# RWKV-5 attention followed by mixture of depths: weight loads re-cut and begun later, u and the gate vector as columns, state products on quarters, one PSUM buffer for the ranking's small results

## The chip, the cores and the metric

The kernel runs on one core of one Trainium2 chip. The metric is the device time in microseconds (us) of one execution; several executions give a median. A profile of one execution shows each instruction with its start, length and what it waited for.

## The reference

```python
batch, n_heads, seq, head_dim = (4, 8, 768, 48)
for t in range(S):
    kt, vt, rt = (k[:, :, t], v[:, :, t], r[:, :, t])
    cur = np.einsum('bhd,bhe->bhde', u[None] * kt, vt)
    y[:, :, t] = np.einsum('bhd,bhde->bhe', rt, state + cur)
    state = w[None, :, :, None] * state + np.einsum('bhd,bhe->bhde', kt, vt)
...
x = np.ascontiguousarray(attn_out.transpose(0, 2, 1, 3)).reshape(B, S, H * D)
scores = np.einsum('bsd,d->bs', x, w_gate)
out = x.copy()
for b in range(B):
    top_idx = np.argpartition(-scores[b], capacity)[:capacity]
    xe = x[b, top_idx]
    ye = np.maximum(xe @ w1, 0.0) @ w2
    g = 1.0 / (1.0 + np.exp(-scores[b, top_idx]))
    out[b, top_idx] = x[b, top_idx] + g[:, None] * ye
```

A linear recurrence per head, then, for the 128 (capacity) best tokens of each batch, an expert with 1024 hidden values (w1 is 384 x 1024, w2 is 1024 x 384). All data are float32.

## The kernel before

Time is cut into 24 units of 128 tokens, six per batch (NU = 24, NC = 6), each with all 8 heads in 4 pairs. The main loop (L571) handles unit n as follows; each engine runs its instructions in program order.

- PE: `states(n - 1)` (L312, what the state adds to y), `products(n)` (L277, key times value: what each half of the unit adds to the state), `scores(n)` (L286, key times query inside the unit), `values(n - 1)` (L331, scores times values), `turn(n + 1)` (L254, transposes of key and query), then ranking and expert work that the plan has put there.
- DVE: `added(n, 0)` (L299), `masked(n)` (L295), `added(n, 1)`, `turned(n + 1)`, `bonus_sum(n + 1)`, `score(n - 1)` (L366, the gate score), then comparisons for the ranking.
- POOL: `scaled(n + 2)` (L233, kw), `diagonal(n + 1)` (L251, at), `bonus(n + 2)` (L237 rk, L243 rku). About four instructions of 1.0 us or more in each unit.
- ACT: copies out of PSUM, the decay of the state (L310), the copy of y into x (L353 to L357).
- SP: issues nearly all DMAs, in order. `load(n + 4, part)` is held behind an instruction of unit n (the first `added`, `masked`, `turned`, `bonus_sum`), the weights behind `masked` and `score`, and the store of a unit's x behind ACT's copies. r, k and v come in rows of 192 bytes.

The products of a pair of heads (L282) use all 128 tokens as the contraction at once. The value tile `vpad` has 2 x 48 columns per head: the first half of the tokens has its values in the left 48 and zeros in the right, the second half the other way round, so that one product gives the sums of both halves side by side. The sums lie in the last 192 columns of the two PSUM banks of `rp`, the scores in the first 256.

[...] `rp` takes two, `y0` and `y1` two, and four go round under the name "m": transposed keys (pk) and queries (pr) in each unit, the transposed score row (`scores_along`, L375), the rank sums (`rank`, L396), the picked token numbers (`pick`, L434), the hidden layer (PH) and the expert's sum (PE, held over three units).

`plan(b)` (L528) puts the expert part of batch b on the units after it, with n = 6(b + 1): the score rows up to unit n + 1, the rank sums (`rank`) and the one-hot rows (`match`) in unit n + 2 ("turn"), `pick` and `fetch` (an indirect DMA on POOL's queue) in unit n + 3 ("bonus"), `chosen` in unit n + 5, then 8 hidden and 8 expert parts by MOVE: hidden 0 to 3 in unit n + 5, 4 and 5 in n + 6, 6 and 7 in n + 7, expert 0 to 2 in n + 8, 3 to 5 in n + 9, the last two in n + 10. Within a unit, "bonus" comes before "turn" and "turn" before "end". For the last batch all this is written out at the kernel's end.

`weights(j, behind)` (L166) loads piece j: pieces 0 to 7 are 128 hidden columns of w1 (all three row blocks, rows of 512 bytes), pieces 8 to 15 are 128 rows of w2 (1536 bytes each). Unit n issues pieces 2(n - 6) and 2(n - 6) + 1, that is in units 6 to 13. u and w_gate come as one row that is sent to all 128 partitions (L129, L557).

Before the loop, ACT clears the unused halves of `vpad` 2 to 5 (L153), PE runs 14 warm-up matmuls around `turn(0)`, and DVE makes the tables of powers of w.

Of the kernel before, what the change touches and what calls it, by code (L numbers as in the profile page):

```python
# [7 lines left out]
F32 = mybir.dt.float32  # L8
# [9 lines left out]
def kernel(  # L18
# [55 lines left out]
    for i, q in enumerate((nc.sync, nc.scalar)):  # L74
        q.dma_start(
            out=wp[i * PAD : i * PAD + D, 0, :],
            in_=bass.AP(tensor=w.tensor, offset=w.offset + i * D, ap=[[1, D], [2 * D, NP]]),
        )
    nc.scalar.activation(mark, mark, AF.Sigmoid)
    busy = const.tile([128, 512], BF16)  # L80
    nc.vector.memset(busy, 0.0)
# [34 lines left out]
    def held(dma, behind):  # L116
        if behind is not None:
            tc.add_manual_dep(dma.ins, behind.ins.name, wait_for, reason="loads come one by one")
# [7 lines left out]
            nc.gpsimd.memset(x[h * C : (h + 1) * C, :, (1 - h) * D : (2 - h) * D], 0.0)  # L126
    load(0, 0)
    load(0, 1)
    nc.sync.dma_start(out=ub, in_=bass.AP(tensor=u.tensor, offset=u.offset, ap=[[0, 128], [D, H], [1, D]]))  # L129
    load(0, 2)  # L130
    load(0, 3)
    load(1)
# [1 line left out]
    def warm(k):  # L134

        p = psum.tile([128, 512], F32, name="m", bufs=4)
        for _ in range(k):
            nc.tensor.matmul(out=p, lhsT=busy[:, :128], rhs=busy, start=True, stop=True)

    w1 = const.tile([128, KD, F], F32)  # L140
    w2 = const.tile([128, FB, Dm], F32)
# [6 lines left out]
    for x in rpads[2:]:  # L148
# [1 line left out]
    rp = psum.tile([128, 2, 512], F32, name="rp")  # L150
    nc.scalar.copy(rp[:, :, NP * C : NP * (C + D)].rearrange("t a (p d) -> t a p d", p=NP),
                   zt[:, None, :, :].to_broadcast([128, 2, NP, D]))
    for x in vpads[2:]:  # L153
        for h in range(2):
            rows = slice(h * C, (h + 1) * C)
            nc.scalar.copy(x[rows, :, (1 - h) * D : (2 - h) * D].rearrange("t (a p) d -> t a p d", a=2),  # L156
                           zt[rows, None, :, :].to_broadcast([C, 2, NP, D]))
    mask = const.tile([128, C], F32)
    dia = const.tile([128, C], F32)
    for c in range(2):  # L160
# [3 lines left out]
    causal = mask.bitcast(U32)[:, None, None, :].to_broadcast([128, 2, NP, C])  # L164

    def weights(j, behind):  # L166
        if 0 <= j < FB:
            f = slice(j * 128, (j + 1) * 128)
            held(nc.sync.dma_start(out=w1[:, :, f], in_=moe_w1.rearrange("(kd p) f -> p kd f", p=128)[:, :, f]), behind)
        elif FB <= j < 2 * FB:  # L170
            f = slice((j - FB) * 128, (j - FB + 1) * 128)
            held(nc.sync.dma_start(out=w2[:, j - FB, :], in_=moe_w2[f, :]), behind)


    tables = const.tile([128, 2, NP, T], F32)
# [98 lines left out]
    def turned(n, pr):  # L274
        return nc.vector.tensor_mul(RH[n][:CH], pr[:CH], tr[:CH])  # L275

    def products(n):  # L277

        for hp in range(NP):
            for i in range(2):  # L280
                at = NP * C + hp % 2 * 2 * D
                nc.tensor.matmul(out=rp[i * PAD : i * PAD + D, hp // 2, at : at + 2 * D],  # L282
                                 lhsT=kws[n % 3][:, 2 * hp + i, :D], rhs=VIN[n][:, 2 * hp + i, :],
                                 start=True, stop=True)

    def scores(n):  # L286
        for hp in range(NP):
# [11 lines left out]
    def added(n, c):  # L299
        z = ZA[n] if c == 0 else ZB[n]  # L300
        g = work.tile([128, NP, D], F32, name=f"g{c}", bufs=3)
        sums = rp[:, :, NP * C : NP * (C + D)].rearrange("d b (p e) -> d b p e", p=2)
        op = nc.vector.tensor_add(g.rearrange("d (b p) e -> d b p e", p=2), sums[:, :, :, c * D : (c + 1) * D],  # L303
                                  z.rearrange("d (b p) e -> d b p e", p=2))
        if c == 0:
            ZB[n] = g
            return op
        ZA[n + 1] = work.tile([128, NP, D], F32, name="z", bufs=3)
        for hp in range(NP):
            nc.scalar.activation(ZA[n + 1][:, hp, :], g[:, hp, :], AF.Copy, scale=wc[:, hp : hp + 1])  # L310
# [54 lines left out]
    def score(n):  # L365
        b, c = divmod(n, NC)  # L366
        return nc.vector.scalar_tensor_tensor(scr, xa[b][:, c, :], 1.0, wg, op0=OP.mult, op1=OP.mult,  # L367
                                              accum_out=sc[b][:, c : c + 1])
# [3 lines left out]
    spacer = const.tile([1, 1], F32)  # L372
    out_rows = out.rearrange("b s d -> (b s) d")

    def scores_along(b, j):  # L375
        p = psum.tile([128, 512], F32, name="m", bufs=4)
        nc.tensor.transpose(p[:, :128], sc[b][:, j : j + 1].to_broadcast([128, 128]), ident)
        SR[b, j] = p[:, :128]
        nc.scalar.copy(along[b % 2][:, j * 128 : (j + 1) * 128], SR[b, j])
# [16 lines left out]
    def rank(b):  # L396


        p = psum.tile([128, 512], F32, name="m", bufs=4)
        nc.tensor.matmul(out=p[:, NC - 1 : NC], lhsT=GT[b][:, 0, :128], rhs=ones[:, 1:2], start=True, stop=True)  # L400
        for c in range(NC - 1):
            for j in range(c + 1, NC):
                nc.tensor.matmul(out=p[:, c : c + 1], lhsT=GT[b][:, j, c * 128 : (c + 1) * 128], rhs=ones[:, 0:1],
                                 start=(j == c + 1), stop=(j == NC - 1))
        q = work.tile([128, NC], F32, name="qq")
        nc.vector.tensor_sub(q, QQ[b], p[:, :NC])
        QQ[b] = q
# [24 lines left out]
                nc.vector.tensor_scalar(oh[:, c, :], slots, q[:, c : c + 1], None, op0=OP.is_equal)  # L432

    def pick(b, z):  # L434
        p = psum.tile([128, 512], F32, name="m", bufs=4)
        for c in range(NC):
            nc.tensor.matmul(out=p[:, :5], lhsT=OH[b, z][:, c, :], rhs=tok[:, b * NC + c, :],
                             start=(c == 0), stop=(c == NC - 1))
        IDX[b, z] = work.tile([128, 1], I32, name="idx", bufs=NST + 1)
        with nc.allow_low_precision(reason="whole numbers below 2^24"):  # L440
            nc.vector.tensor_reduce(IDX[b, z], p[:, :2], axis=AX.X, op=OP.add)
        GA[b, z] = work.tile([128, 1], F32, name="gate", bufs=NST + 1)
        picked = work.tile([128, 1], F32, name="picked")
        nc.vector.tensor_reduce(picked, p[:, 2:5], axis=AX.X, op=OP.add)
        nc.scalar.activation(GA[b, z], picked, AF.Sigmoid)
# [71 lines left out]
    def step(n, where, f, *a):  # L517
        fill.setdefault((n, where), []).append((f, a))
# [9 lines left out]
    def plan(b):  # L528
        n = (b + 1) * NC
        for j in range(NC):  # L530
            step(n - NC + j + 2, "turn", scores_along, b, j)
            step(n - NC + j + 2, "turn", compare, b, j)
        step(n + 1, "turn", count, b)
        step(n + 1, "turn", parts_of_scores, b)
        step(n + 2, "turn", rank, b)
        for z in range(NST):
            step(n + 2, "turn", match, b, z)
            step(n + 3, "bonus", pick, b, z)
            step(n + 3, "bonus", fetch, b, z)
            step(n + 5, "scores", chosen, b, z)  # L540
        parts = [p for z in range(NST) for p in mlp(b, z)]
        for i, (f, a) in enumerate(parts):
            step(n + 5 + MOVE[i * 16 // len(parts)], "end", f, *a)
# [6 lines left out]
            f(*a)  # L550

    bonus(0)
    warm(10)
    pr = turn(0, k0, key_table)
    warm(4)
    load(2)
    nc.sync.dma_start(out=wg, in_=bass.AP(tensor=moe_w_gate.tensor, offset=moe_w_gate.offset, ap=[[0, 128], [1, Dm]]))  # L557
    load(3)
    turned(0, pr)
    bonus_scaled(0, nc.vector)  # L560
# [8 lines left out]
    scaled(1)  # L569
    bonus(1)  # L570
    for n in range(NU):  # L571
        if n == 2:
            late_tables()
        b, c = divmod(n, NC)
        if c == 0:
            ZA[n] = zt
        if n:
            behind = states(n - 1)
        products(n)
        scores(n)  # L580
        work_at(n, "scores")
        load(n + 4, 0, added(n, 0))
        op = masked(n)
        load(n + 4, 2, op)
        weights(2 * (n - NC), op)
        if n:
            values(n - 1, behind)
            finish(n - 1)
        if n + 1 < NU:
            pr = turn(n + 1)  # L590
        if c < NC - 1:
            added(n, 1)
        if n + 1 < NU:
            load(n + 4, 1, turned(n + 1, pr))
            load(n + 4, 3, bonus_sum(n + 1))
        if n + 2 < NU:
            scaled(n + 2)
        if n + 1 < NU:
            diagonal(n + 1)
        work_at(n, "bonus")  # L600
        if n + 2 < NU:
            bonus(n + 2)
        if n:
            weights(2 * (n - NC) + 1, score(n - 1))
        work_at(n, "turn")
        if n + 1 < NU:
            work_at(n, "end")
# [13 lines left out]

    some(2 * NST)
    behind = states(NU - 1)
    scores_along(last, NC - 2)
    compare(last, NC - 2)
    values(NU - 1, behind)
    finish(NU - 1)
    score(NU - 1)
    some(3 * NST)
    scores_along(last, NC - 1)  # L630
    compare(last, NC - 1)
    count(last)
    parts_of_scores(last)
    some(3 * NST)
    rank(last)
    for z in range(NST):
        match(last, z)
    some(2 * NST)
    for z in range(NST):
        pick(last, z)  # L640
        fetch(last, z)
    some(len(before) - NST)
# [38 lines left out]
```

## Time and profile before

| | |
|---|---|
| median of 3 runs | 164.13 us (163.67 to 168.28) |
| the profiled execution | 165.25 us, span 163.5 us |
| PE busy | 146.2 us (89%) |
| POOL busy | 117.7 us (72%) |
| DVE busy | 111.9 us (68%) |
| ACT busy | 76.5 us (47%) |
| DMA packets | 84323, of which 76480 under 512 B; 24.50 MB |
| SP's own queue of loads and stores | 62.8% of 16 engines' span |
| mean granted TensorE clock | 0.996 |

The span runs from the program's first instruction to its last. A busy share is a mean over stages with different limits. A row of a group tells the line, the engine, what is written from what, the shapes and the count, then busy us, mean ns of one, and the idle time just before. In a timeline, the first number is the start in us from the span's start, the second the length, and brackets at the end tell the idle time before an instruction and what ended it. In the chain of waits, each line is a start, a length and the engine and line that held up the end.

### The profile page before, as it was taken

To read this page: it belongs to the slowest core of one execution; us is meant where nothing else is said; L and a number is where in the kernel's file an instruction comes from. 1 tells how busy PE (TensorE), PEld (TensorE's weight loads), DVE (VectorE), ACT (ScalarE), POOL (GpSimd) and SP (SyncE) were. 2 spreads that over 40 slices of the span, in tenths; PEclk is the share of its full clock that TensorE was granted. 3 is DMA by queue.
4 is the path that set the end of the run, shared out by engine and by line. 5 is a ranking of instruction groups with operands and counts; after the bars stand their busy time and mean duration, and the time that the engine had idled before them with its cause. 6 is when DMAs were issued, how large, how long until landed. Compare 5 with 4: busy or idle time off the path is not lost.

```text
span 163.5 us, 7873 instructions
## 1 busy us (share of the span) xinstructions
PE 146.2 (89%) x3278; PEld 119.2 (73%) x3278; DVE 111.9 (68%) x352; ACT 76.5 (47%) x251; POOL 117.7 (72%) x156
## 2 busy tenths in 40 slices
PE   6969979997998866999998999999989999999970
PEld 2558868885787756999875779999676788858830
DVE  7856768889999956797898387488984857701010
ACT  6816666545664645167516344546643645102100
POOL 8499999999999996878799979688978431122002
PEclk9999999999999999999999999999999999999998
DMA  4998788888989989998999999988502212011001
GB/s 76 193 193 162 134 185 155 183 178 181 202 193 190 210 212 222 217 214 220 227 226 232 232 184 219 211 170 195 122 4 62 88 52 100 0 48 52 0 0 48
DMA packets 84323, 24.50 MB, mean 150 GB/s; under 512 B 76480, under 2 KB 83904, under 8 KB 84288
## 3 DMA queue, kind: packets, MB, share of 16 engines
q1 hardware_dynamic: 83568, 22.42, 62.8%
q0 software_dynamic: 512, 1.57, 2.9%
q8 instruction: 26, 0.43, 1.1%
q14 instruction: 9, 0.07, 0.1%
q10 hardware_dynamic: 208, 0.00, 0.1%
HBM read 18.48 MB, written 5.51 MB: 147 GB/s over the span
## 4 chain that ended last, share of the span: by engine, by line
PE 49%; POOL 20%; issue 13%; ACT 7%; DMA 6%; DVE 2%; POOLq 1%; SPq 0%; ACTq 0%; DVEq 0%
PE m L480 10%; PE m L489 7%; PE rp L282 7%; PE y L322 5%; PE rp L292 5%; POOL at L251 5%; PE m L260 4%; PE y L338 4%; POOL kw L233 4%; POOL rk L237 4%; POOL rku L243 4%; PE m L265 4%; DMA kin<-in_k_dram 3%; DMA rpad<-in_r_dram 3%; ACT vpad L156 2%
## 5 line engine op out<-in xcount | busy, mean ns | idle before, releaser
L251 POOL TENSOR_TENSOR at<-dia,du 128x512 f32<-128x512 f32 x24 | 30.0, 1249 | 7.4 <-DVE du L247 3.6
L237 POOL TENSOR_TENSOR rk<-rpad,kin 128x384 f32<-128x384 f32 x23 | 23.1, 1005 | 3.0 <-DMA rpad<-in_r_dram 2.9
L233 POOL TENSOR_TENSOR kw<-kin,wk 128x384 f32<-128x384 f32 x23 | 23.8, 1035 | 1.8 <-DMA kin<-in_k_dram 1.7
L243 POOL TENSOR_TENSOR rku<-rk,ub 128x384 f32<-128x384 f32 x23 | 23.1, 1004 | 1.8
L282 PE MATMUL rp<-vpad,kw 128*48 128x96 f32 x384 | 21.6, 251 | 2.9 <-POOL kw L233 1.2
L480 PE MATMUL m<-xt,w 128*128 128x128 f32 x192 | 23.2, 276 | 0.0
L489 PE MATMUL m<-w,ht 128*128 128x384 f32 x64 | 22.7, 492 | 0.1
L480 PEld LDWEIGHTS m<-xt,w 128*128 128x128 f32 x192 | 22.3, 192 | 0.6 <-ACT xt L471 0.5
L310 ACT ACTIVATE z<-g,wp 128x48 f32<-128x48 f32 x80 | 20.2, 325 | 4.8 <-DVE g L303 4.8
L355 ACT COPY x<-y 128x192 f32<-128x192 f32 x24 | 7.7, 320 | 27.4 <-PE y L338 26.6
L282 PEld LDWEIGHTS rp<-vpad,kw 128*48 128x48 f32 x384 | 16.3, 122 | 5.0 <-POOL kw L233 1.7
L275 DVE TENSOR_TENSOR rh<-m,tables 112x512 f32<-112x512 f32 x24 | 16.5, 686 | 4.5 <-PE m L265 4.5
L367 DVE SCALAR_TENSOR_TENSOR scr<-x,wg 128x384 f32<-128x384 f32 x24 | 17.9, 747 | 1.8 <-ACT x L357 1.8
L297 DVE COPY_PREDICATED at<-mask,rp 128x512 f32<-128x512 uint32 x24 | 17.6, 735 | 1.6 <-POOL at L251 1.6
L322 PE MATMUL y<-g,rh 48*64 48x48 f32 x384 | 16.7, 222 | 2.1 <-issue 1.2
L247 DVE TENSOR_REDUCE du<-rku 128x8 f32<-128x384 f32 x24 | 13.2, 549 | 6.5 <-POOL rku L243 6.3
L322 PEld LDWEIGHTS y<-z,rh 48*64 48x64 f32 x320 | 12.4, 134 | 6.8 <-issue 5.2
L292 PE MATMUL rp<-rh,kh 48*64 48x64 f32 x768 | 16.7, 224 | 0.0
L260 PE MATMUL m<-ident,kw 128*112 128x128 f32 x92 | 14.9, 285 | 1.8 <-POOL kw L233 1.8
L322 PE MATMUL y<-z,rh 48*64 48x48 f32 x320 | 15.7, 223 | 0.9 <-issue 0.9
L389 DVE TENSOR_SCALAR_CACHE_REDUCE gt<-along,sc 128x128 bf16<-128x128 f32 (+5 forms) x24 | 16.2, 676 | 0.2 <-issue 0.2
L292 PEld LDWEIGHTS rp<-rh,kh 48*64 48x64 f32 x768 | 13.4, 134 | 3.7 <-issue 0.7
(95 smaller groups left out, 250.7 us busy)
## 6 DMA issues: line engine op xcount, KB each, us to landing
rpad<-in_r_dram SPq DMA_DIRECT2D x24, 192.0 KB, 3.4
vpad<-in_v_dram SPq DMA_DIRECT2D x48, 96.0 KB, 4.4
out_dram<-x SPq DMA_DIRECT2D x24, 192.0 KB, 3.7
kin<-in_k_dram SPq DMA_DIRECT2D x23, 192.0 KB, 3.8
w<-in_moe_w_dram SPq DMA_DIRECT2D x16, 192.0 KB, 4.3
k<-in_k_dram SPq DMA_DIRECT2D x1, 192.0 KB
ub<-in_u_dram SPq DMA_DIRECT2D x1, 192.0 KB, 4.4
wg<-in_moe_w_gate_dram SPq DMA_DIRECT2D x1, 192.0 KB
```

What stands on the lines that cost most here:

```text
L233: nc.gpsimd.tensor_mul(kws[n % 3][:, :, :D], KIN[n], wk)
L237: nc.gpsimd.tensor_mul(rk, rpads[n % NIN][:, :, :D], KIN[n])
L243: engine.tensor_mul(RKU[n], RK[n], ub)
L251: nc.gpsimd.tensor_mul(AT[n], dia[:, None, :].to_broadcast([128, H, C]), DU[n].rearrange("t i p -> t (i p)")[:, :, None].to_broadcast([128 ...
L260: nc.tensor.transpose(pk[:CH, hp, :], two_heads(kws[n % 3] if keys is None else keys, hp), ident)
L282: nc.tensor.matmul(out=rp[i * PAD : i * PAD + D, hp // 2, at : at + 2 * D], lhsT=kws[n % 3][:, 2 * hp + i, :D], rhs=VIN[n][:, 2 * hp + i, ...
L292: nc.tensor.matmul(out=rp[ts, i, hp * C : (hp + 1) * C], lhsT=KH[n][rows, hp, ts], rhs=RH[n][rows, hp, ts], start=True, stop=True)
L310: nc.scalar.activation(ZA[n + 1][:, hp, :], g[:, hp, :], AF.Copy, scale=wc[:, hp : hp + 1])
L322: mm = nc.tensor.matmul(out=YP[n][i][j * C : (j + 1) * C, hp * D : (hp + 1) * D], lhsT=RH[n][rows, hp, c * C : (c + 1) * C], rhs=z[rows, h ...
L367: return nc.vector.scalar_tensor_tensor(scr, xa[b][:, c, :], 1.0, wg, op0=OP.mult, op1=OP.mult, accum_out=sc[b][:, c : c + 1])
L480: nc.tensor.matmul(out=ph[:, f % 4, :], lhsT=w1[:, d, f * 128 : (f + 1) * 128], rhs=XT[b, z][:, d, :], start=(d == 0), stop=(d == KD - 1))
L489: nc.tensor.matmul(out=pe[:, :Dm], lhsT=HT[b, z][:, f, :], rhs=w2[:, f, :], start=(f == 0), stop=(f == FB - 1))
```

## The change

The pieces of w1 are re-cut: six of 128 rows x 512 columns (2 KB per row, 256 KB each), one for each row block and half of the hidden columns. w2 stays in eight. The 14 pieces go out in units 8 to 15 by a table: one in unit 8, two in 9, one in 10 and two in each of 11 to 15; the first of a unit behind `masked`, the second behind `score`. The hidden parts 0 to 3 use the first three pieces, 4 to 7 the next three.

u and w_gate come as 128 x 3 columns, u over ACT's queue and w_gate over POOL's; PE's transposes spread a column over all partitions (`to_all`), and DVE (u) or ACT (w_gate) copies the result out of PSUM. The clearing of `vpad` 4 and 5 moves behind that copy, and the warm-up matmuls become 6 + 3 + 3.

In the last batch (units 18 to 23) `products` runs one product for each half of the tokens, with a contraction of 64 and 48 columns; each half of the tokens writes into its own bank. `added` reads accordingly.

`side()` gives one "m" buffer per loop iteration, shared by score row (columns 0 to 127), ranks (128 on) and picked (192 on). `rank` and `match` move from "turn" to "end" of their unit, behind expert parts of an earlier batch.

```diff
+    columns = const.tile([128, 2, KD], F32)
+    for i, (x, q) in enumerate(((u, nc.scalar), (moe_w_gate, nc.gpsimd))):
+        q.dma_start(out=columns[:, i, :], in_=bass.AP(tensor=x.tensor, offset=x.offset, ap=[[1, 128], [128, KD]]))
...
-    nc.sync.dma_start(out=ub, in_=bass.AP(tensor=u.tensor, offset=u.offset, ap=[[0, 128], [D, H], [1, D]]))
...
+    def to_all(i):
+
+        p = psum.tile([128, 512], F32, name="m", bufs=4)
+        for d in range(KD):
+            nc.tensor.transpose(p[:, d * 128 : (d + 1) * 128], columns[:, i, d : d + 1].to_broadcast([128, 128]), ident)
+        return p[:, :Dm]
...
+        if j < F // 512 * KD:
+            f, d = slice(j // KD * 512, (j // KD + 1) * 512), j % KD
+            held(nc.sync.dma_start(out=w1[:, d, f], in_=moe_w1[d * 128 : (d + 1) * 128, f]), behind)
+        else:
+            f = j - F // 512 * KD
+            held(nc.sync.dma_start(out=w2[:, f, :], in_=moe_w2[f * 128 : (f + 1) * 128, :]), behind)
+
+    NWP = F // 512 * KD + FB
+    DUE = {}
+    for j in range(NWP):
+        DUE.setdefault(2 * NC - 4 + (0, 1, 1, 2, 3, 3, 4, 4, 5, 5, 6, 6, 7, 7)[j * 14 // NWP], []).append(j)
...
+                if quarters(n):
+                    for c in range(2):
+                        ts, at = slice(c * C, (c + 1) * C), NP * C + hp * D
+                        nc.tensor.matmul(out=rp[to, c, at : at + D], lhsT=kws[n % 3][ts, h, :D],
+                                         rhs=VIN[n][ts, h, c * D : (c + 1) * D], start=True, stop=True)
...
+        if quarters(n):
+            op = nc.vector.tensor_add(g, sums[:, c].rearrange("d (p e) -> d p e", p=NP), z)
...
+    def side():
+
+        if 0 not in SIDE:
+            SIDE[0] = psum.tile([128, 512], F32, name="m", bufs=4)
+        return SIDE[0]
+
     def scores_along(b, j):
-        p = psum.tile([128, 512], F32, name="m", bufs=4)
+        p = side()
...
-        p = psum.tile([128, 512], F32, name="m", bufs=4)
+        p = side()[:, 128 : 128 + NC]
...
-        p = psum.tile([128, 512], F32, name="m", bufs=4)
+        p = side()[:, 192 : 192 + 5]
...
-        step(n + 2, "turn", rank, b)
+        step(n + 2, "end", rank, b)
         for z in range(NST):
-            step(n + 2, "turn", match, b, z)
+            step(n + 2, "end", match, b, z)
...
-    warm(10)
+    warm(6)
+    nc.vector.tensor_copy(ub, to_all(0).rearrange("t (h d) -> t h d", h=H))
+    warm(3)
     pr = turn(0, k0, key_table)
-    warm(4)
+    nc.scalar.copy(wg, to_all(1))
+    for x in vpads[4:]:
+        cleared(x)
+    warm(3)
...
     for n in range(NU):
+        SIDE.clear()
...
-        weights(2 * (n - NC), op)
+        weights_due(n, True, op)
...
-            weights(2 * (n - NC) + 1, score(n - 1))
+            weights_due(n, False, score(n - 1))
```

At the kernel's end `SIDE.clear()` stands ahead of each of the last batch's steps, so that there every step has a buffer of its own, as before.

More of the change, by code (lines that the diff above doesn't have):

```diff
@@ L152, with cleared @@
                    zt[:, None, :, :].to_broadcast([128, 2, NP, D]))
-    for x in vpads[2:]:
+    def cleared(x):
         for h in range(2):
@@ L157 @@
                            zt[rows, None, :, :].to_broadcast([C, 2, NP, D]))
+    for x in vpads[2:4]:
+        cleared(x)
     mask = const.tile([128, C], F32)
@@ L166, in weights, with weights_due @@
     def weights(j, behind):
[L167 to L172, printed above, removed]
+        if j < F // 512 * KD:
[8 more added lines that the diff above has]
+        DUE.setdefault(2 * NC - 4 + (0, 1, 1, 2, 3, 3, 4, 4, 5, 5, 6, 6, 7, 7)[j * 14 // NWP], []).append(j)
+    def weights_due(n, first, behind):
+        for j in DUE.get(n, [])[:1] if first else DUE.get(n, [])[1:]:
+            weights(j, behind)
     tables = const.tile([128, 2, NP, T], F32)
@@ L275, in turned, with quarters @@
         return nc.vector.tensor_mul(RH[n][:CH], pr[:CH], tr[:CH])
+    def quarters(n):
+        return n >= NU - NC
     def products(n):
@@ L280, in products @@
             for i in range(2):
[L281 to L284, printed above, removed]
+                h, to = 2 * hp + i, slice(i * PAD, i * PAD + D)
+                if quarters(n):
[3 more added lines that the diff above has]
+                                         rhs=VIN[n][ts, h, c * D : (c + 1) * D], start=True, stop=True)
+                else:
+                    at = NP * C + hp % 2 * 2 * D
+                    nc.tensor.matmul(out=rp[to, hp // 2, at : at + 2 * D], lhsT=kws[n % 3][:, h, :D],
+                                     rhs=VIN[n][:, h, :], start=True, stop=True)
     def scores(n):
@@ L301, in added @@
         g = work.tile([128, NP, D], F32, name=f"g{c}", bufs=3)
-        sums = rp[:, :, NP * C : NP * (C + D)].rearrange("d b (p e) -> d b p e", p=2)
-        op = nc.vector.tensor_add(g.rearrange("d (b p) e -> d b p e", p=2), sums[:, :, :, c * D : (c + 1) * D],
-                                  z.rearrange("d (b p) e -> d b p e", p=2))
+        sums = rp[:, :, NP * C : NP * (C + D)]
+        if quarters(n):
+            op = nc.vector.tensor_add(g, sums[:, c].rearrange("d (p e) -> d p e", p=NP), z)
+        else:
+            sums = sums.rearrange("d b (p e) -> d b p e", p=2)[:, :, :, c * D : (c + 1) * D]
+            op = nc.vector.tensor_add(g.rearrange("d (b p) e -> d b p e", p=2), sums,
+                                      z.rearrange("d (b p) e -> d b p e", p=2))
         if c == 0:
@@ L373 @@
     out_rows = out.rearrange("b s d -> (b s) d")
+    SIDE = {}
+    def side():
+        if 0 not in SIDE:
+            SIDE[0] = psum.tile([128, 512], F32, name="m", bufs=4)
+        return SIDE[0]
     def scores_along(b, j):
-        p = psum.tile([128, 512], F32, name="m", bufs=4)
+        p = side()
         nc.tensor.transpose(p[:, :128], sc[b][:, j : j + 1].to_broadcast([128, 128]), ident)
@@ L552 @@
     bonus(0)
-    warm(10)
+    warm(6)
+    nc.vector.tensor_copy(ub, to_all(0).rearrange("t (h d) -> t h d", h=H))
+    warm(3)
     pr = turn(0, k0, key_table)
-    warm(4)
+    nc.scalar.copy(wg, to_all(1))
+    for x in vpads[4:]:
+        cleared(x)
+    warm(3)
     load(2)
-    nc.sync.dma_start(out=wg, in_=bass.AP(tensor=moe_w_gate.tensor, offset=moe_w_gate.offset, ap=[[0, 128], [1, Dm]]))
     load(3)
@@ L623 @@
     behind = states(NU - 1)
+    SIDE.clear()
     scores_along(last, NC - 2)
@@ L629 @@
     some(3 * NST)
+    SIDE.clear()
     scores_along(last, NC - 1)
@@ L634 @@
     some(3 * NST)
+    SIDE.clear()
     rank(last)
@@ L639 @@
     for z in range(NST):
+        SIDE.clear()
         pick(last, z)
```

## The prediction

> **What bounds the kernel now.** I read the page's 40 slices first, for which engine is full where.
>
> ```profile
> POOL 8499999999999996878799979688978431122002
> DMA  4998788888989989998999999988502212011001
> ```
>
> A slice is 4.1 us. POOL is full up to slice 14, the DMA engines up to slice 28. Then the chain that ended last, in order of time, shows where one hands over to the other.
>
> ```profile
> 49.84 1.01 POOL kw L233
> 50.89 0.65 PE m L260 x4
> ...
> 58.87 4.62 DMA rpad<-in_r_dram
> 63.49 0.14 issue
> 63.63 0.62 PE m L265 x4
> 64.36 2.68 PE m L480 x24
> ...
> 70.65 1.34 PE m L480 x12
> ...
> 102.13 0.61 PE y L322 x32
> 102.74 0.80 PE rp L282 x16
> 103.54 0.62 PE rp L292 x32
> 104.16 0.45 PE y L338 x32
> ```
>
> POOL up to 51 us, one wait for a load of r at 58.87, and from 63.63 PE without a gap: one unit is states (L322), products (L282), scores (L292), values (L338), turn (L260, L265) and expert work. L480 at 64.36 is hidden parts 0 to 3 (unit 11), at 70.65 parts 4 and 5 (unit 12). SP's own timeline gives the pace of the loads.
>
> ```profile
> 16.40 0.55 SPq L114 DMA_DIRECT2D kin<-in_k_dram  x1
> 42.81 0.69 SPq L114 DMA_DIRECT2D kin<-in_k_dram  x1
> 66.37 0.43 SPq L114 DMA_DIRECT2D kin<-in_k_dram  x1
> 76.62 0.70 SPq L172 DMA_DIRECT2D w<-in_moe_w_dram  x1
> 88.03 0.91 SPq L114 DMA_DIRECT2D kin<-in_k_dram  x1
> ```
>
> These are the loads of k for units 4, 10, 14 and 18. A unit without weights takes (42.81-16.40)/6 = 4.40 us of the queue, with two w1 pieces (66.37-42.81)/4 = 5.89, with two w2 pieces (88.03-66.37)/4 = 5.41. So a w1 piece costs 0.74 and a w2 piece 0.51. The queue is late: k of unit 14 is released by the first `added` of unit 10 (DVE L303 at 56.21) and issued at 66.37. SP hardly idles, and single issues last up to 2.8 us, so transfers set its pace. Last, the waits on PSUM.
>
> ```profile
> DVE g L303 <- PE rp L292: 12.4, 12, 2.5
> ```
>
> `added` reads only product columns of rp, yet it waits for the scores, which write other columns of the same banks. [...]
>
> ```profile
> 86.64 0.29 PE L437 MATMUL m<-tok,oh 128*128 128x5 bf16 x6
> 87.46 0.32 PE L377 MATMUL m<-ident,sc 128*128 128x128 f32 x1 [0.53 <-ACT kh L270]
> 88.17 0.15 DVE L444 TENSOR_REDUCE picked<-m 128x1 f32<-128x3 f32 x1
> ```
>
> This is unit 15, the PE and DVE timelines: the score row's transpose (L377) waits 0.53 for a free buffer; DVE reads what pick (L437) wrote only at 88.17.
>
> [...] the same four transposes take 0.58 behind the 64-row values (L260) and 0.44 behind themselves (L265), so a switch costs about 0.14. [...] no plain DMA from GpSimd is in this trace.
>
> **The change, part by part**, against the execution with span 163.5 us (its own time 165.25, the median of three runs 164.13; I add the sum to the median).
>
> *Weights.* Before, 16 pieces go out in units 6 to 13; after, six w1 pieces of 256 KB (units 8 to 11: 1, 2, 1, 2) and eight of w2 (units 12 to 15). Up to r of unit 12, five w1 pieces become one, so the wait at 63.49 goes: PE idle there was 1.31, gain up to 1.4. But deadlines shrink. The third piece of w1's second half is issued at the end of unit 11, and hidden part 4 needs it at the end of unit 12. Before, that place in the queue was the issue at 76.62. From it: minus u and w_gate, 0.85+0.62 = 1.47 of SP issue (bounds 0.5, if transfers hide part of the issue, and 3, if each of the two costs two w1 pieces); minus the pieces ahead of it then, 8 x 0.74 + 3 x 0.51 = 7.45; plus five new pieces ahead. Each has 128 rows as a w2 piece has: 0.51 if rows count, 0.68 if bytes do at w2's rate, 0.99 at w1's. I take 0.51, as rows of 1.5 and 2 KB are near. 76.62-1.47-7.45+2.55 = 70.25, and with w's median landing of 4.3, 74.55. PE needs it at its third product, 70.65+0.45 = 71.1 in the old time. PE stalls: +3.45. Behind it on PE is everything: the next states, products, turn. The last w2 piece is late by less: old place about 97.2, minus 1.47, minus 10.0, plus 6 x 0.51 + 7 x 0.51 = 6.6, gives 92.3+4.3 = 96.6, needed at 94.55+3.45.
>
> *Start.* u and w_gate come as 128x3 columns, transposed by PE. PE runs 6 warm matmuls (0.43 each, to 3.8), then waits for u (the similar w columns were issued at 0.91 and used at 3.24; u, issued at 1.35, some 0.7 later and longer: 4.4), then 3 transposes of 0.15 and 3 warms of 1.28 in all: turn at 6.1, before 5.36. POOL issues w_gate's DMA ahead of iota jp: nearest row, an indirect issue on POOL, 1.0; bounds 0.3 and 2. DVE's ident and tables shift as much, beside the PE delay; DVE adds a copy of 0.4. I take +0.9 for POOL's first `at` (9.02), bounds -0.3 (wk's copy no longer sits behind eight ACT copies of 0.51) and +1.5. It is covered while loads are late. The ACT copy of wg (0.48) and four clears move into ACT's idle 3.92 ahead of L270 at 11.75; without that, 2.5.
>
> *One PSUM buffer, ranks at the end.* By bank, L377 now waits until DVE has read picks. Unit 15: 88.25 against 87.46, +0.85; unit 21: DVE reads until 123.2 against 122.56, +0.75. Units 14 and 20: ranks follow the experts, but must wait for DVE's compare (L387, behind `score`): -0.2 (buffer wait gone) and +0.1. Unit 8 has no expert work: PE stands from 46.9 until L387, which is behind `score` (49.02 to 49.57), so to about 50.1; behind it are states, products and turn of unit 9, which waited 0.44 for POOL anyway. Unit 9 adds a wait for picks. Followed through DVE (full there: 4.96 of 5.0 us), PE reaches unit 11's hidden parts at 63.8 instead of 64.36: it eats 0.85 of the 1.4. Sum for units 14 to 21: +1.5.
>
> *Quarters, units 18 to 23.* 8 products of 128 rows x 96 columns (0.80, 16 records) become 16 of 64 rows x 48 (32 records). The nearest row is values: 32 records of 48 columns, 0.45. Scores then follow without a mode switch, 0.62 less up to 0.14. Saved per unit: 0.19 (if they cost as states, 0.61), 0.35, or 0.48. PE is the bound in all six: 0.40 x 6 = -2.4, bounds -1.1 and -2.9.
>
> Sum: +3.45+1.5-2.4 = +2.55. 164.13+2.55 = 166.7.
>
> **Rivals.** A is this forecast. B, weights come in time (u and w_gate worth 3 us, the queue catching up at 4.1 a unit): unit 12 then ends at -0.55+0.9, total +0.35+1.5-2.4 = -0.55: 163.6. For it: releases are then nearly the bound, about 69.7 for the landing. Against: SP was late by 5 us in every early unit. C, faster: loads cease to bind, start and unit 8 stay hidden, PE keeps the whole 1.4: -1.4+1.6-2.9 = -2.7, 161.4. Against: unit 8's PE wait. D, slower, one mechanism: a 256 KB piece is priced by bytes at w1's rate, 0.99. The piece is then issued at 72.65 and lands at 76.95: stall 5.85, total +4.95, 169.1. It passes 2% from a price of 0.66. For it: w1's landing pace. Against: w2's rows, three times longer than w1's, came at less.
>
> **Numbers.** A 0.44 (own range 164.8 to 168.5), B 0.22, C 0.12, D 0.22. Range 162.0 to 170.0 leaves out half of C, and the top of D and A. A measurement of this kernel can tell about 2% (160.8 and 167.4) from no change. Faster: half of C and a little of B, 0.08. Slower: D and 0.14 of A, 0.36. Same: 0.56.
>
> **What would show it.** Unit 12: L480 waiting for DMA w at about 72 to 75 confirms A; no wait there refutes it. L377 in units 15 and 21 must wait for DVE picked, and PE in unit 8 for DVE scr L387; if not, banks aren't tracked as I say. L282 in units 18 to 23 near 0.45 per unit. L237 and L265 without a DMA wait near 63. A queue pace well under 4.4 us in units 8 to 12 would make the prediction too slow.

## The result and the profile after

The changed kernel takes 172.70 us (median of four runs, 172.31 to 176.63), the kernel before 165.07 in the same comparison: ratio 1.048, interval 1.036 to 1.061. It is slower, and slower than the predicted range of 162 to 170. The profiled execution took 172.31 us with a span of 170.4, so 6.9 more than the span before. Medians here and below are over all executions, while ratios and intervals leave out the executions that ran in a slower state, which any of these kernels enters at times.

The 40 slices of the page after, one of them 4.26 us:

```profile
POOL 7699999999999199958199496969996740222002
PEclk9999999999995699997899999999999999999999
DMA  4998998887698598999497887868611112110001
```

Before, POOL was full without a hole up to slice 14 and the clock row was all nines up to its last slice. Now POOL stands almost still in the 14th and the 20th slice, and TensorE's granted clock is down in the 13th and 14th (0.5 and 0.6) and again in the 19th and 20th (0.7 and 0.8). PE's timeline shows what stands ahead of both:

```profile
51.43 0.16 PE L449 MATMUL m<-ones,gt 128*128 128x1 bf16 x1 [3.48 <-DVE scr L436]
52.97 1.52 PE L320 MATMUL rp<-vpad,kw 128*48 128x96 f32 x16
59.63 0.32 PE L426 MATMUL m<-ident,sc 128*128 128x128 f32 x1 [1.24 <-DVE picked L493]
77.16 1.16 PE L529 MATMUL m<-xt,w 128*128 128x128 f32 x8 [1.74 <-DMA w<-in_moe_w_dram]
78.91 1.52 PE L320 MATMUL rp<-vpad,kw 128*48 128x96 f32 x16
96.49 0.32 PE L426 MATMUL m<-ident,sc 128*128 128x128 f32 x1 [1.25 <-DVE picked L493]
```

The first rank sum of batch 0 waits 3.48 in unit 8 for DVE's compare, the score rows in units 9 and 15 for DVE's reading of the picks, hidden part 4 in unit 12 for a piece of w1. Behind the two long waits the same 16 products (L320) span 1.52 instead of 0.87. The chain that ended last passes through the same places:

```profile
51.02 0.37 DVE scr L436 x2
52.00 1.04 PE y L363 x25
53.03 1.45 PE rp L320 x16
...
73.05 4.07 DMA w<-in_moe_w_dram
77.16 1.16 PE m L529 x8
...
111.20 0.36 PE rp L316 x32
111.56 0.48 PE rp L329 x32
```

The last two lines are the quarters of unit 18 and their scores: 0.84 where the chain before had 0.80 + 0.62 = 1.42. SP's timeline, loads of k for units 4, 10, 14 and 18:

```profile
13.30 0.55 SPq L117 DMA_DIRECT2D kin<-in_k_dram  x1
39.46 0.74 SPq L117 DMA_DIRECT2D kin<-in_k_dram  x1
63.14 0.38 SPq L117 DMA_DIRECT2D kin<-in_k_dram  x1
87.30 0.38 SPq L117 DMA_DIRECT2D kin<-in_k_dram  x1
```

Up to unit 10 the queue is 3 us ahead of the old one at the same pace, (39.46 - 13.30)/6 = 4.36. Most of that lead is gone by unit 18 (87.30 against 88.03), because k of a unit is released by DVE's `added`, and those come late now. The waits for rp's banks are as before in kind (first line: us in all, times, the longest); PE's wait for the shared buffer is new (second line):

```profile
DVE g L344 <- PE rp L329: 15.2, 10, 3.8
PE m L449 <- DVE scr L436: 4.2, 2, 3.5
```

The starts of `states` in PE's timeline tell where the 6.9 us arise (differences of starts, in us):

| stretch | before | after | difference |
|---|---|---|---|
| start of unit 1 | 12.08 | 13.65 | +1.57 |
| units 1 to 7 | 30.45 | 30.12 | -0.33 |
| unit 8 (waits 3.48) | 4.74 | 8.16 | +3.42 |
| unit 9 (slow clock, waits 1.24) | 4.93 | 7.96 | +3.03 |
| units 10 and 11 | 14.77 | 11.40 | -3.37 |
| unit 12 (waits 1.74) | 4.95 | 6.96 | +2.01 |
| unit 13 (slow clock) | 4.95 | 6.45 | +1.50 |
| units 14 to 17 | 25.19 | 25.82 | +0.63 |
| units 18 to 23 (quarters) | 32.62 | 30.88 | -1.74 |
| the rest | 28.8 | 29.0 | +0.2 |

### The profile page after: what moved, and what is told of

It reads as the page before. It is cut to its first block, busy times and chain, and to the rows that moved or that the text cites. A ratio compares the mean times of both kernels' runs of the same rounds, so it can differ in the third digit from the quotient of the medians.

```text
span 170.4 us, 8074 instructions
## 1 busy us (share of the span) xinstructions
PE 147.5 (87%) x3378; PEld 121.8 (71%) x3378; DVE 110.5 (65%) x353; ACT 77.1 (45%) x252; POOL 118.5 (70%) x157
## 3 DMA queue, kind: packets, MB, share of 16 engines
q0 software_dynamic: 544, 1.57, 2.8%
## 4 chain that ended last, share of the span: by engine, by line
PE 46%; DVE 15%; POOL 15%; issue 12%; DMA 6%; ACT 1%; SPq 1%; POOLq 1%; DVEq 0%; ACTq 0%
PE m L529 7%; PE y L363 6%; PE rp L329 5%; PE y L379 5%; PE m L286 5%; PE m L538 5%; PE rp L320 5%; PE m L291 4%; POOL rku L269 4%; DMA rpad<-in_r_dram 4%; POOL at L277 3%; POOL kw L259 3%; DVE du L273 3%; DVE rh L301 2%; DVE scr L408 2%
## 5 line engine op out<-in xcount | busy, mean ns | idle before, releaser
L379 PE MATMUL y<-vpad,at 64*64 64x48 f32 x768 | 17.0, 225 | 1.5 <-issue 1.3
L363 PE MATMUL y<-g,rh 48*64 48x48 f32 x384 | 17.3, 226 | 1.1 <-DVE g L344 0.5
L320 PE MATMUL rp<-vpad,kw 128*48 128x96 f32 x288 | 16.9, 264 | 1.4 <-POOL kw L259 1.1
L329 PE MATMUL rp<-rh,kh 48*64 48x64 f32 x768 | 17.4, 231 | 0.0
L408 DVE SCALAR_TENSOR_TENSOR scr<-x,wg 128x384 f32<-128x384 f32 x24 | 15.9, 661 | 1.9 <-ACT x L398 1.8
L379 PEld LDWEIGHTS y<-vpad,at 64*64 64x64 f32 x768 | 14.9, 142 | 2.4 <-issue 2.2
L286 PE MATMUL m<-ident,kw 128*112 128x128 f32 x92 | 15.4, 291 | 1.4 <-POOL kw L259 1.4
L363 PEld LDWEIGHTS y<-z,rh 48*64 48x64 f32 x320 | 12.9, 138 | 4.6 <-issue 3.0
L329 PEld LDWEIGHTS rp<-rh,kh 48*64 48x64 f32 x768 | 14.3, 141 | 2.6 <-issue 0.5
```

The lines of the kernel that those rows point to most:

```text
L286: nc.tensor.transpose(pk[:CH, hp, :], two_heads(kws[n % 3] if keys is None else keys, hp), ident)
L320: nc.tensor.matmul(out=rp[to, hp // 2, at : at + 2 * D], lhsT=kws[n % 3][:, h, :D], rhs=VIN[n][:, h, :], start=True, stop=True)
L329: nc.tensor.matmul(out=rp[ts, i, hp * C : (hp + 1) * C], lhsT=KH[n][rows, hp, ts], rhs=RH[n][rows, hp, ts], start=True, stop=True)
L363: mm = nc.tensor.matmul(out=YP[n][i][j * C : (j + 1) * C, hp * D : (hp + 1) * D], lhsT=RH[n][rows, hp, c * C : (c + 1) * C], rhs=z[rows, h ...
L379: mm = nc.tensor.matmul(out=YP[n][i][j * C : (j + 1) * C, hp * D : (hp + 1) * D], lhsT=AT[n][ts, i * NP + hp, :], rhs=VIN[n][ts, 2 * hp + ...
```

## The experiments

Theory: two things delay PE, each by its wait and again by a slow clock behind it: the shared PSUM buffer (unit 8) and the late dates of the weight pieces (units 11 to 15). Rivals: the pieces wait only because the buffer has made everything late; the width of the new pieces, not their date, is at fault; the slow clock has another cause than PE's standing still. All ratios are to the kernel before, run beside on the same chip.

| kernel | median | ratio | interval |
|---|---|---|---|
| changed kernel | 172.70 | 1.048 | 1.036 to 1.061 |
| e1 own buffers | 168.37 | 1.031 | 1.020 to 1.043 |
| e2 buffer alone | 170.60 | 1.038 | 1.022 to 1.054 |
| e3 quarters alone | 163.50 | 0.992 | 0.988 to 0.996 |
| e4 filled wait | 169.74 | 1.027 | 1.013 to 1.040 |
| e5 own buffers, early pieces | 162.61 | 0.985 | 0.974 to 0.996 |
| e6 columns alone | 164.05 | 0.996 | 0.989 to 1.003 |
| e7 buffer alone, filled | 168.68 | 1.024 | 1.015 to 1.033 |
| e8 quarters, early pieces | 163.99 | 0.986 | 0.975 to 0.998 |
| e9 pieces alone | 172.81 | 1.050 | 1.039 to 1.061 |
| e10 shared buffer, early pieces | 168.56 | 1.028 | 1.016 to 1.040 |
| e11 as e5, columns on ACT | 163.65 | 0.991 | 0.987 to 0.995 |
| e12 as e11, ranks at the turn | 163.42 | 0.991 | 0.988 to 0.994 |

**e1, own buffers.** The changed kernel, in `scores_along`, `rank` and `pick`:

```diff
-        p = side()
+        p = psum.tile([128, 512], F32, name="m", bufs=4)
```

> The changed kernel, but score row, ranks and picked each take a buffer of their own again (ranks stay at the end of the unit). Bank theory: the 3.48 us wait of PE for DVE scr in unit 8, the waits for picked in units 9, 15 and 21 and the low clock of units 9 go; unit 10 starts about 7.7 us earlier, at 53 to 54 us instead of 59.9, and the time falls by 5 us or more, below 168. Weights theory: the deadline of the third piece of w1's second half then binds by itself, PE waits 3 us or more for w in unit 12, and the time stays above 169.

Unit 8 and 9 lose their waits; unit 10 starts at 53.74 instead of 59.89. The time falls by 4.3 us, a little less than expected, and stays well above that of the kernel before. The rival's wait for w1 in unit 12 doesn't come: the piece is issued at 68.93. Other waits come up:

```profile
62.73 0.55 PE L518 MATMUL m<-ident,xr 128*128 128x128 f32 x3 [2.38 <-DMA xr<-out_dram,idx]
92.64 0.91 PE L538 MATMUL m<-w,ht 128*128 128x384 f32 x2 [1.74 <-DMA w<-in_moe_w_dram]
```

The first is for the picked rows that `fetch` brings, the second for a piece of w2, and the clock goes down behind both, to 0.63 and 0.76 in the 3 us that follow. So late transfers are a cost of their own, hidden in the changed kernel by the lateness of PE. That the rows come late because of the pieces isn't shown: in e11, whose pieces are early, PE waits 2.79 for them.

**e2, the buffer alone**: the kernel before with `side()` and ranks and matches at "end".

> The kernel before with only the shared buffer and the ranks at the end. Bank theory: PE waits 3 us or more for DVE scr in unit 8, the clock falls in unit 9, and unit 10 starts 5 to 7 us later than before; part of that is given back where PE waited for r of unit 12, and 1.5 us come on top in units 15 and 21: ratio 1.03 to 1.05. Weights theory: the loads of before are all in time, so at most 1 us more: ratio 1.00 to 1.01.

```profile
49.85 0.16 PE L408 MATMUL m<-ones,gt 128*128 128x1 bf16 x1 [3.48 <-DVE scr L395]
51.39 1.52 PE L282 MATMUL rp<-vpad,kw 128*48 128x96 f32 x16
58.06 0.32 PE L385 MATMUL m<-ident,sc 128*128 128x128 f32 x1 [1.24 <-DVE picked L452]
```

The same waits and the same slow products without any other part of the change, and most of the lost time.

**e4 and e7, the wait filled.** PE runs filler matmuls ahead of the ranks of batch 0, in e4 nine on the changed kernel, in e7 thirteen on e2, with five more behind the pick:

```diff
+        if b == 0:
+            warm(13)
```

> The changed kernel with nine matmuls of the warm-up kind, whose result nobody reads, on PE ahead of the rank sums of batch 0, so that PE works through the wait of unit 8. If PE's standing still is what lowers the clock, the clock stays near 1.00 from 52 to 60 us, the states-to-turn part of unit 9 takes 3.5 us instead of 6.3, and unit 10 starts 2 to 3 us earlier; the time falls by 1 to 3 us. If the clock falls for another reason (power, the number of matmuls), it falls here too and the time stays or rises.

> The kernel before with the shared PSUM buffer and the ranks and matches at an iteration's end (as the buffer-alone run), and with 13 filler matmuls (0.264 us each) ahead of the ranks of batch 0 and 5 behind its pick, so that PE works through the 3.5 us and the 1.2 us in which it otherwise stands for the compare and the picked copy. Their result is not used. Theory, clock: the wait itself stays as filler time (3.4 us), but the granted clock stays above 0.9 from 48 to 64 us, unit 9 takes at most 6 us instead of 8, and the time falls 2 to 4 us below the buffer-alone run (170.6), ratio about 1.02. Rival: the clock falls for another reason than PE's standing still, or the slow stretch is DVE's, and the time stays within 1 us of 170.6.

In e4 a filler took 0.264 us, 2.11 for the eight that the trace has; 1.30 us of standing still stayed, and the clock from 52 to 56 was 0.59. That decides nothing about the clock. The wait for w1 in unit 12 grew to 2.41. In e7 the fillers (L138) fill most of the wait:

```profile
46.41 2.97 PE L138 MATMUL m<-busy 128*128 128x512 bf16 x12
50.03 0.16 PE L410 MATMUL m<-ones,gt 128*128 128x1 bf16 x1 [0.66 <-DVE scr L395]
51.11 0.87 PE L282 MATMUL rp<-vpad,kw 128*48 128x96 f32 x16
```

Here are the windows from 52 to 56 us of the changed kernel and then of e7; the column behind POOL's is the granted clock.

```profile
52.00:56.00 4.00, 4.00 (x108) 3.66 (x112) 2.23 (x15) 0.19 (x1) 3.92 (x5) 0.50 0.84 206
```

```profile
52.00:56.00 4.00, 3.80 (x100) 2.82 (x104) 3.50 (x13) 2.72 (x10) 3.29 (x4) 1.00 0.81 197
```

Unit 8 is as long as in e2 (8.46), so the wait is still paid. But unit 9 takes 5.20 instead of 7.96, with the clock from 52 to 56 at 1.00 instead of 0.50: with PE at work through the wait, the slow clock of unit 9 is gone. The ratio falls from 1.038 to 1.024; the intervals overlap, so the gain rests on the profiles: unit 12 starts 2.0 earlier than in e2 (68.45 against 70.42), and 1.0 of it is left in the span (167.4 against 168.4).

**e9, the pieces alone**: the kernel before with the 14 pieces in units 8 to 15.

> The kernel before with the 14 wider weight pieces at the changed kernel's units (8 to 15) alone: start, buffers, ranks and products as before. Theory, dates: the pieces issued with units 12 to 15 are needed at once, so PE waits for a w1 piece in unit 12 or for a w2 piece in unit 15, 1.5 to 3.5 us, with a slow clock of some 4 us behind it that costs 1 to 2 us more: 167 to 169 us, ratio 1.015 to 1.03. Rival: with nothing else late the pieces arrive in time, as the queue is lighter in units 6 and 7, and the ratio is 0.995 to 1.005.

```profile
65.83 4.13 PE L507 MATMUL m<-xt,w 128*128 128x128 f32 x20 [2.02 <-DMA w<-in_moe_w_dram]
76.56 2.08 PE L507 MATMUL m<-xt,w 128*128 128x128 f32 x8 [2.54 <-DMA w<-in_moe_w_dram]
```

```profile
76.00:80.00 4.00, 3.44 (x46) 3.13 (x48) 0.41 (x2) 0.19 (x1) 2.93 (x4) 0.54 0.94 226
80.00:84.00 4.00, 4.00 (x87) 3.66 (x84) 1.23 (x3) 0.92 (x3) 0.00 (x0) 0.60 0.11 32
```

Twice PE waits for w1, in unit 11 for the first half's third piece and in unit 12 for the second half's, and twice the clock goes down behind it, to 0.55 and to 0.50 in the 3 us that follow. Unit 11 takes 12.59 (9.98 before), unit 12 8.67 (4.95), unit 13 6.93 (4.95). It costs more than I expected, as much as the whole change. (The profiled execution took 174.44, 1.6 above its median.) So the pieces are waited for without the buffer too; the first rival falls.

**e5 and e10, the pieces two units earlier**, in e1 and in the changed kernel:

```diff
-        DUE.setdefault(2 * NC - 4 + (0, 1, 1, 2, 3, 3, 4, 4, 5, 5, 6, 6, 7, 7)[j * 14 // NWP], []).append(j)
+        DUE.setdefault(NC + (0, 1, 1, 2, 3, 3, 4, 4, 5, 5, 6, 6, 7, 7)[j * 14 // NWP], []).append(j)
```

> The changed kernel with a PSUM buffer each for score row, ranks and picked (as in the run before), and with the 14 weight pieces issued two units earlier, behind units 6 to 13. Theory, lateness of the pieces' own dates: unit 12 and unit 15 no longer wait for a piece of w1 or w2, unit 15 takes about 6.4 us instead of 8.4, the clock stays above 0.9 in unit 16, and the time falls 2 to 4 us below that of the own-buffer run (168.4), to 166 or less, ratio at most 1.015. Rival: the queue only moves its lateness onto the r loads, PE then waits over 1 us for a padded r in units 10 to 14, and the time stays within 1 us of 168.4.

> The changed kernel with the 14 pieces issued two units earlier alone (units 6 to 13); the shared PSUM buffer and all else as changed. Theory: the two costs stand apart. The wait of 3.5 us in unit 8 and the slow clock in unit 9 stay, the weight wait of unit 12 goes: 167.5 to 170, ratio 1.015 to 1.03, 2 to 5 us below the changed kernel. Rival: the weight wait of the changed kernel only comes from the lateness that the buffer made, so that nothing but 0 to 1 us is won and the ratio stays at 1.04 or more.

In e5 no piece is waited for, hidden parts 0 to 3 begin at 63.40, and the clock is all nines up to the tail; it is the fastest kernel of the study. In e10 the wait in unit 8 remains (3.00) and unit 12 has none. The four kernels stand in a square: shared and late 1.048, own and late 1.031, shared and early 1.028, own and early 0.985. The pieces keep their width in e5 and e10, so the date is at fault; the second rival falls too.

**e3 and e8, the quarters** on the kernel before, in e8 with early wide pieces.

> The kernel before with only the state products of units 18 to 23 on quarters. By the trace of the changed kernel products and scores of a unit take 0.36 + 0.48 = 0.84 us instead of 0.80 + 0.62 = 1.42: six units by 0.58 give -3.5 us, ratio 0.979. If other engines or buffers then bind in these units, half of it or less: ratio above 0.989.

> The kernel before with the quarters in the last batch and the 14 weight pieces (w1 rows of 2 KB, w2 rows of 1.5 KB) at units 6 to 13; start, PSUM buffers and ranks as before. Theory: the quarters give about 0.58 us a unit, 2 to 3 us in the last six units, and the pieces in fewer and longer rows cost nothing where they come early: 161 to 162.5 us, ratio 0.98 to 0.99. Rival: a piece of 14 to the half is larger and holds the r loads of units 10 to 13 longer than the smaller ones before, a wait for a padded r of 1 to 2 us comes back, and the ratio is 0.99 to 1.005.

Both gain, though the ratio of e8 rests on two executions. In e3 units 18 to 23 take 30.78 instead of 32.62, less than expected: unit 20 lost 1.43 us in a gap between rank sums that no semaphore explains.

```profile
114.93 0.23 PE L418 MATMUL m<-ones,gt 128*128 128x1 bf16 x3 [1.43 <-issue]
```

Such a gap isn't chance. All nine traces with quarters have one of 0.95 to 1.99 us in unit 20 or 21; the five without have none over 0.4 there. The gaps lie at two places in PE's stream of instructions, behind about 5445 records in four traces and 5697 in five. Each ends 2.3 to 2.9 us after a packet of 16 KB started on the queue that the page calls "q8 instruction". The changed kernel has 27 such packets for 6756 records of PE, so 250 records each, and the two places lie about 250 apart. That PE waits there for its own instructions, as it runs through them faster than before, is my guess from these counts; no run tests it.

**e6, e11, e12, start and place of the ranks.** e6 is the kernel before with the columns; e11 is e5 with both columns on ACT's queue, e12 the same with ranks and matches back at "turn".

```diff
-    for i, (x, q) in enumerate(((u, nc.scalar), (moe_w_gate, nc.gpsimd))):
+    for i, (x, q) in enumerate(((u, nc.scalar), (moe_w_gate, nc.scalar))):
```

> The kernel before with the new start alone: u and w_gate read as columns on ACT's and POOL's queues and spread by TensorE, the broadcast loads gone. Theory, start: POOL's first turn product comes at about 10.6 us instead of 9.0 because the column DMA holds POOL's next instruction, unit 1 starts about 13.6 instead of 12.1, and as no later wait covers it while the loads arrive on their dates, 1 to 2 us of it reach the end: ratio 1.005 to 1.012. Rival: the loads of units 1 to 3 are what is late there anyway, two broadcast loads fewer make them earlier, and the ratio is 0.99 to 1.00.

> The changed kernel with own PSUM buffers and early pieces (the run of 162.6 us), and both column loads on ACT's queue, so that POOL's iota isn't held by one. Theory: iota of jp back at 0.85 us, ident 1.4 us earlier, POOL's first turn product at 9.3 to 9.7 us instead of 10.6, unit 1 at 12.3 to 12.8 instead of 13.65; as unit 3 then meets the loads, 0.3 to 1.2 us are left at the end, 161.4 to 162.3. Rival: the second column load on ACT holds ACT's table load instead and the end doesn't move, within 0.3 us of 162.6.

> As the run before it (own buffers, early pieces, both columns on ACT's queue), with the rank sums and matches back beside the turn. Theory: with a buffer of their own the ranks' place is worth under 0.5 us either way, 161.4 to 162.7. Rival: ranks at the turn stand for the compare ahead of the products and cost about 1 us in units 8, 14 and 20 together.

POOL's timeline in e6:

```profile
1.30 0.93 POOL L81 DMA_DIRECT2D columns<-in_moe_w_gate_dram  x1 [0.84 <-POOLq L681]
2.32 0.27 POOL L86 IOTA jp<- 128x128 f32 x1
10.57 1.05 POOL L264 TENSOR_TENSOR at<-dia,du 128x512 f32<-128x512 f32 x1
```

POOL issues the column load for 0.93 us and the iota comes at 2.32 instead of 0.85; its first `at` is 1.55 late. Unit 1 starts 1.56 later, but hidden parts 0 to 3 begin at 63.75 instead of 64.19: the rival's ratio held. Not its place, though: units 8 and 11 still start 1.1 and 1.2 later, and the delay goes in unit 11, where the wait for r is gone. Two broadcast loads fewer would explain that; no run tests it alone.

In e11 the iota is back at 0.85 and `at` at 9.87, short of the expected 9.3 to 9.7. ACT's table load starts 0.66 later, as the rival had it, but so it does in e12, where `at` comes at 9.07 and unit 1 at 12.15. So the table load isn't what holds `at` in e11. Unit 1 of e11 starts at 12.94, but unit 3 takes 6.84 (5.17 in e5): PE stands 1.45 there, again with no semaphore, 2.5 us after a packet of q8 started. Then it waits 2.79 for the picked rows in unit 11. (The profiled execution took 165.91, 2.3 above its median.) In e12 a start 1.5 earlier than in e5 is still worth 1.7 at unit 10 and nothing at unit 18. No gain shows in either median, though a difference of 1 us can't be told across two comparisons. e11 and e12 agree within their intervals: with buffers of their own, the ranks' place is worth nothing measurable.

## Why the prediction was wrong

The sum was +2.55, the span grew by 6.9. Of the 4.4 between, 2.9 had arisen by the start of unit 13 (78.25 against 71.92, so 6.3 where 3.45 was forecast) and 1.5 in unit 13. Behind it +1.5 - 2.4 = -0.9 was forecast and -0.9 measured, in part by luck: the quarters gave more than forecast, unit 14 and a gap in unit 21 took it back.

**Unit 8** is the first failed step. The place and the wait were right: PE stood until 51.4 for the compare, 3.48 us (forecast about 50.1, in the time of before). What failed is "it eats 0.85 of the 1.4", that PE would reach the hidden parts of unit 11 at 63.8. The changed kernel reaches them at 68.52. I counted on DVE as the bound that would take up the wait, and on a wait costing its own length. e7 shows the first error alone, at full clock: 65.68, against 64.19 before. The other is the slow clock. Unit 9 took 7.96 with it and 5.20 without: 2.8 us that the sum didn't contain. I had not asked what PE does after 3 us of standing still: behind the 3.48 us here the clock was 0.50 for 6.83 us, and behind the 1.74 us of unit 12 it was 0.50 for 3.41 us (the last section has the windows).

**Weights** is the second: the date of the piece that hidden part 4 reads. It was forecast to go out at 70.25 and to land at 74.55; it went out at 73.05 and landed at 77.12. The sum took the queue for the late party all the way, so that only the loads ahead of the piece count. In the changed kernel SP itself waits, ahead of k of unit 14 at 63.14, for `added` of unit 10, late from unit 8 (SP's waits from 60 to 74 us):

```profile
SPq L117 <- DVE g L344: 2.2, 1, 2.2
```

The price of a piece isn't what failed. Without the shared buffer the piece went out at 68.93 in e1, 1.3 ahead of the sum. In e9 u and w_gate stay in the queue, so there the sum is 76.62 - 7.45 + 2.55 = 71.72, and the piece went out at 72.15. Rival D has 72.65 for the changed kernel, which is near, but by luck: its price would give 74.12 in e9. The price isn't fixed either. In e9 the loads of k for units 10 and 14 are issued at 42.12 and 62.89, at a pace of (42.12 - 16.41)/6 = 4.29 without pieces; three pieces lie between, so one took (62.89 - 42.12 - 4 x 4.29)/3 = 1.2. In e5, with six pieces between the same loads (40.53 and 62.26) and a pace of (40.53 - 13.32)/6 = 4.54 ahead of them, the same sum gives 0.6. So an average taken over one stretch of the queue doesn't date a single transfer in another.

Two terms were missing. In unit 11 the wait for r was to go, a gain of up to 1.4, and in e9 a wait of 2.02 for the third piece of the first half stands in its place: I had looked at the deadline of the second half alone. (In the changed kernel PE comes too late to meet that one.) And the slow clock again: unit 13 takes 1.98 more in e9, 1.50 more in the changed kernel.

That the changed kernel isn't as slow as both costs together (0.038 + 0.050 - 0.008 - 0.004 = 0.076 against 0.048) fits the table: while PE stands in unit 8, the queue catches up so far that SP waits, and units 10 and 11 win back 3.37. PE then stood 1.74 for the piece in unit 12 instead of the 3.45 of the forecast, though the piece landed later.

**Start**: forecast +0.9 for POOL's first `at`, measured +1.6, just above the upper bound. That it is covered while loads are late was right (e6, 0.996).

**One buffer, units 14 to 21**: the score rows waited for DVE's picks, as forecast (1.25 us each in units 15 and 21). Whether such a dependence goes by bank or by buffer these runs don't tell; that it goes by bank was my reading of the waits for rp. Unit 15 lost 0.72 (forecast 0.85, though 88.25 - 87.46 is 0.79; 123.2 - 122.56 for unit 21 is 0.64, not 0.75) and unit 20, with its quarter, took 0.48 less. Unit 21 lost 1.3 with its quarter (0.75 was forecast before it): the gap of 0.95 that came with the quarters stands on top. Unit 14 lost 0.47, where -0.2 was forecast: behind the expert parts PE still waited 0.74 for DVE's compare. It did so in all five traces with the shared buffer (0.4 to 0.9), and not in e1.

**Quarters**: 0.84 against 1.42 is 0.58 per unit, more than the 0.40 of the sum and above its upper bound (0.48): the products take 0.36, less than the values row's 0.45, and the scores behind them 0.48 instead of 0.62. That is 0.14 less, as much as lies between the transposes' 0.58 and 0.44 in the prediction; that both come from a switch of mode was my estimate, and no run tests it. Units 18, 19, 22 and 23, where no rank or pick is waited for, each took 0.55 to 0.77 less. The one gap of 0.95 to 1.99 that came with the quarters takes part of it back; the sum had no term for it.

## What to carry to other kernels

A stretch in which TensorE stands still has to be priced with the slow matmuls behind it: here ten of the eleven of 1.73 to 3.48 us had a clock of 0.50 to 0.79 behind them, and the two in the changed kernel cost 2.8 and 1.5 us in the unit that follows (9 and 13). Of the 28 shorter ones, three had a lowered clock behind them. A wait that sits in front of a queue of the engine that binds later isn't swallowed because another engine is full there: follow it to the next place where both meet. And when pieces of a transfer are re-cut and dated later, look for every piece's first reader, not for the last one's only; here the date cost 2 to 5%, the cut itself nothing that shows. Last, a finer cut of matmuls means more instructions in less time (here 32 records in 0.36 us instead of 16 in 0.80), and a wait of 0.95 to 1.99 us with no semaphore came with it in all nine traces that have it.

## What the runs showed of the hardware that I had not expected

I took from all fourteen traces each stretch behind the first 10 us in which TensorE neither multiplied nor loaded weights for over 1.0 us, and the granted clock in the 3 us behind it:

| PE stood for | cases | clock behind it |
|---|---|---|
| 1.03 to 1.29 us | 23 | 1.00 in 22; 0.82 in one, 7 us behind a wait of 3.48 |
| 1.30 to 1.65 us | 5 | 1.00 in three, 0.70 and 0.71 in two |
| 1.73 to 3.48 us | 11 | 0.50 to 0.79 in ten; 1.00 in one (1.99 us, in e8) |

Why 1.74 was enough in one place and 1.99 not in another, the clock's own record in the traces shows. It changes only on a grid: in all fourteen traces each stretch at one clock, up to the last, lasts a whole multiple of 3.41 us (44.37 = 13 x 3.413 in the changed kernel, then 6.83 at half, 20.48 at full, 3.41 at half). So in these traces the clock held for 3.41 us or a multiple of it at a time. The windows of 3.41 us around the wait in unit 8 and the one in unit 12 of the changed kernel (PE's busy time stands behind the length, the clock behind POOL's):

```profile
48.03:51.44 3.41, 0.01 (x1) 0.01 (x1) 3.26 (x11) 1.57 (x6) 3.04 (x8) 1.00 0.85 181
51.44:54.86 3.42, 3.42 (x80) 3.06 (x83) 2.05 (x15) 0.19 (x1) 3.34 (x4) 0.50 0.81 202
54.86:58.27 3.41, 3.41 (x74) 3.26 (x66) 1.23 (x3) 1.78 (x6) 1.29 (x2) 0.50 0.57 117
75.34:78.75 3.41, 1.68 (x41) 1.47 (x40) 2.35 (x8) 1.20 (x6) 2.47 (x3) 1.00 1.00 255
78.75:82.16 3.41, 3.41 (x93) 3.07 (x84) 0.60 (x2) 0.19 (x1) 1.66 (x2) 0.50 0.62 146
```

Laid on this grid, the windows at full clock, without the first and last 10 us of each trace, sort by how long PE was busy in them. Under 1.75 us, all ten were followed by half clock; from 1.96 to 2.18 us, three of 22; above, none of over 500. The 1.74 of unit 12 lies inside one window (1.68 busy). The 1.99 of e8 falls on a border at 116.08, and the windows on its two sides have 2.81 and 2.03. In the changed kernel half clock then lasted one window (3.41 us, behind unit 12) or two (6.83, behind unit 8). The score row's wait of 1.24 left PE busy for about 2.17 and mostly cost its own length alone. Nor does the grid lie at the same place each time: the first full clock is granted at 4.2 to 7.1 us from the start, at another point in nearly every execution. Of the five waits of 1.30 to 1.65 us two were followed by a lowered clock; that it goes by where they fall on the grid is my estimate from these windows.

A small DMA issued by POOL (128 x 3 values) held POOL's next instruction for 0.93 us (e6 and the changed kernel), about as long as an indirect one (0.99 to 1.18 in the kernel before).
